# Chunk-selecting attention with a squared-ReLU feed-forward layer: x transposed by DMA in group 1, squares in pairs, keys placed after the bounds, a smaller causal mask

## The chip, the cores and the metric

The kernel runs on one core of one Trainium2 chip. The core has a matrix engine (TensorE, PE in the profile; its weight loads are shown apart as PEld), a vector engine (VectorE, DVE), a scalar engine (ScalarE, ACT), a general engine (GpSimd, POOL) and a queue engine (SyncE, SP). DMA transfers are issued from the queues of SP, ACT and POOL. Times are device microseconds (us) of the whole program; less is better.

## What is computed

Four sequences of 768 tokens with eight heads of 64 columns go through an attention that looks only at the best six chunks of keys for each query, and the result through a feed-forward layer with squared ReLU.

```python
k_min, k_max = min and max of k over each chunk of 32 keys
ub = sum over d of max(q * k_min, q * k_max)        # one bound per query and chunk
ub = where(chunk is not in the future, ub, -1e9)
top_chunks = the 6 chunks with the largest ub
scores = q @ k.T / 8, kept where the chunk is in top_chunks and the key is not in the future
attn = softmax(scores) @ v
x = attn with heads side by side                     # (3072, 512)
out = maximum(x @ w_in, 0) ** 2 @ w_out              # d_ff = 2048
```

## The kernel before

The work is cut into **groups** and **slots**. A group is one half (384 queries) of one sequence; `ORDER` lists the eight groups, half 0 of sequence 0, half 0 of sequence 1, half 1 of 0, half 1 of 1, then sequence 2 and 3 in order. A slot `s` is one pair of heads (`p` = 0 to 3) of one group, so slots 0 to 3 are group 0, slots 4 to 7 group 1, slots 8 to 11 group 2, and slot 31 is the last. In the code a group's number is `hb` or `g`, and `NP` is 4.

For each slot these steps run, spread over the slots before and after it:

- **step_P** (line 344) transposes keys and queries of the slot on PE (`tk`, `tq`, lines 251 and 258), from group 3 on it reads them from DMA transposes. **step_T2** (263) then makes the two relus of the query on ACT (`qr`, 279), the minimum and maximum of each key chunk on DVE (`extrema`, 218 to 226, into `kbd`) and **places** keys and queries in the operands of the scores (`place`, 281 to 285, `kq`): keys on DVE, queries on ACT.
- **step_U** (353) makes the bounds on PE: a matmul that adds the causal mask (359: identity times `cmask`, 144 columns in a second half, 48 in a first half), then two small matmuls per query block (363). DVE takes the eight largest bounds of each row (MAX8, 370) and writes which chunks fall short of the sixth (`chosen`, `nsel` or `qn`, 371).
- **step_V** (397) brings these choices into the query operand: transposes on PE into `qt` (404, 416), then copies by DVE (410; in slots 4 to 11 one copy for each of the two heads, 421). From slot 13 on **step_W** (390) does it by one DMA transpose issued from SP.
- **step_E** (424) computes scores of a head on PE (`ps`, 434) and their exponential on ACT (`e`, 440); POOL clears the causal triangle (444). **step_F** (450) multiplies by V (`po`, 460) and divides on DVE (`r`, `x`, 469 and 470). From group 2 to group 6 it also issues a DMA transpose of `x` from SP (474) into `xT`.
- Groups 0, 1 and 7 transpose `x` on PE instead (`x_T`, 492 to 501, tile `pt`) and copy it (`x_copy`, 504). For group 1 this stands in slot 8 (two sets of six transposes, g = 0 and 1), for group 7 in **step_X** (506) behind the last slot.
- **push** (513) puts a group's feed-forward pieces in a queue: 16 **ups** (`ffn_up`, 544: four matmuls `ph` against `w_in`, 547; a relu on ACT into `ht`, 551; a square on DVE into `h`, 553) and 12 **downs** (`ffn_down`, 556: four matmuls `py`, 563; each reads four of the 16 `h`). The main loop takes pieces from the queue by `f1()` at fixed places, four in each of slots 4 to 7 and six to eight in each later slot, so that PE has matmuls while the attention steps wait.

Every engine works its instructions off in program order; the order is written out by hand in two loops at the end, one for slots 0 to 3 and one for slots 4 to 31. Tables `later` (`at`, line 583), `first` and `by_sp` say at which slot a load or a DMA transpose is issued. Loads from HBM go through POOL's queue, in the order `at` gives: behind slot 0 both halves of `w_in`, behind slot 1 V of sequence 1, then keys and queries of group 2, then both halves of `w_out`.

Of the kernel before, what the change touches and what calls it, by code (L numbers as in the profile page):

```python
# [8 lines left out]
F32 = mybir.dt.float32  # L9
# [30 lines left out]
def kernel(  # L40
# [131 lines left out]

    cmask = consts.tile([128, HT, 2, NC], BF16, tag="cmask", name="cmask")
    nc.vector.memset(cmask, 0.0)
    for g in range(4):
        for j in range(HT):
            c = 13 + g + 4 * j
            if c < NC:
                nc.vector.memset(cmask[g * 32:(g + 1) * 32, j, :, c:NC], NEG)

# [172 lines left out]
    def step_U(s):  # L353
        b, half, p = slots[s]
        st[s]["e"] = [None, None]
        ncs = 12 * (half + 1)
        j0 = 1 - half
        ub = psA.tile([128, HT - j0, 2, ncs], F32, tag="att", name="ub")
        nc.tensor.matmul(ub, lhsT=ident, rhs=cmask[:, j0:, :, NC - ncs:NC],
                         start=True, stop=False)  # L360
        for j in range(j0, HT):
            for w in range(2):
                nc.tensor.matmul(  # L363
                    ub[:, j - j0], lhsT=st[s]["qr"][:, w, 128 * j:128 * (j + 1)],
                    rhs=kbds[b % 2][:, p, w, :, 0:ncs], start=False,
                    stop=(j == HT - 1 and w == 1))
        m8 = work.tile([128, HT, 2, 8], F32, tag="m8", name="m8")
        for j in range(j0, HT):
            for hh in range(2):
                nc.vector.max(out=m8[:, j, hh, :], in_=ub[:, j - j0, hh, :])  # L370
        nc.vector.tensor_tensor(
            (qn0[:, j0:, p, :, D:D + ncs] if s < NP else
             chosen[s % 2][:, j0:, :, 0:ncs] if s < ON_PE * NP else
             nsel[half][:, s % 2, :, j0:, 1, 0:ncs].rearrange("p h j c -> p j h c")),
            ub, m8[:, j0:, :, TOPK - 1:TOPK].to_broadcast([128, HT - j0, 2, ncs]),
            op=ALU.is_lt)
# [20 lines left out]
    def step_V(s):  # L397
        b, half, p = slots[s]
        if s < NP or s // NP >= ON_PE:

            qt = psA.tile([128, 2, HB], BF16, tag="att", name="qt")
            for hh in range(2):
                for j in range(HT):
                    nc.tensor.matmul(
                        qt[0:KR, hh, 128 * j:128 * (j + 1)],
                        lhsT=(qn0[:, j, p, hh, :] if s < NP else
                              nsel[half][:, s % 2, hh, j].rearrange("r n d -> r (n d)")
                              [:, 0:KR]),
                        rhs=ident, is_transpose=True, start=True, stop=True)
# [40 lines left out]
    def step_F(s, hh):  # L450
# [13 lines left out]
        if hh == 1:  # L464
            if p == 0:
# [14 lines left out]
    downs = []  # L480
    h2 = {}

    xTs = {}
# [22 lines left out]
    def step_X(hb, pe):  # L506
        if pe:
            for g in range(2):
                x_T(hb, g, A)
                x_copy(hb, g, 0, 2, nc.scalar.copy if g else nc.vector.tensor_copy)  # L510
        push(hb)

# [31 lines left out]
    def ffn_up(hb, xT, f):  # L544
        ph = psF.tile([128, 512], F32, tag="ph", name="ph")
        for ki in range(NKI):
            nc.tensor.matmul(  # L547
                ph[:, 0:HB], lhsT=w_in[:, ki, 128 * f:128 * (f + 1)],
                rhs=xT[:, ki, :], start=(ki == 0), stop=(ki == NKI - 1))
        ht = late.tile([128, HB], BF16, tag="ht", bufs=4, name="ht")  # L550
        nc.scalar.activation(ht, ph[:, 0:HB], ACT.Relu)  # L551
        h = late.tile([128, HB], BF16, tag="h", bufs=2 * NFI + 2, name="h")
        nc.vector.tensor_mul(h, ht, ht)  # L553
        h2[hb, f] = h

# [42 lines left out]
    at(0, codes, 1, 0, nc.gpsimd.dma_start)  # L598
    for g in range(2):
# [110 lines left out]
    for s, (b, half, p) in enumerate(slots):  # L710
# [32 lines left out]
        if s == 2 * NP:  # L743
# [7 lines left out]
            step_F(s - 1, 1)  # L751
            f1()
            f1()
            x_T(1, 1, F)
            x_copy(1, 1, 0, 2, nc.scalar.copy)
            push(1)
            extrema(st[s + 1]["k"], s + 1)
            place(s + 1, "k", nc.vector.tensor_copy)
        if p == 0 and hb > 2:
            step_F(s - 1, 0)  # L760
            step_F(s - 1, 1)
            step_X(hb - 1, False)
        else:
# [82 lines left out]
    fill(4, True)  # L846
    step_X(2 * B - 1, True)
    queue.extend(downs)
# [33 lines left out]
```

## Time and profile before

| | us |
|---|---|
| three runs: median (lowest to highest) | 270.51 (270.15 to 272.39) |
| the execution that was profiled | 270.16 |
| its span, first to last instruction | 268.4 |
| PE busy | 257.3 (96%) |
| ACT busy | 179.7 (67%) |
| DVE busy | 162.3 (60%) |
| POOL busy | 90.6 (34%) |

The granted clock of TensorE was 0.999 of full speed. A line of the timeline reads: start, length, engine, line of the code, operation, what it writes and reads, how many instructions are taken together; in brackets stands how long the engine idled before it and what ended that. A line of instructions taken together starts with the first and ends with the last, and one instruction may still be in its pipeline when the next begins; the step from start to start is what it holds its engine. That matters on PE, where a matmul's length in the profile is longer than the step to the next one. In the 40 slices a digit is the busy share in tenths; a slice is 6.7 us.

### The profile page before, as it was taken

How to read it: one execution, taken by the hardware profiler on the slowest of the kernel's cores; microseconds unless marked ns; L12 is line 12 of the kernel's file. 1: busy time of each engine (PE TensorE's matmuls, PEld its weight loads, DVE VectorE, ACT ScalarE, POOL GpSimd, SP SyncE). 2: the span in 40 equal slices, each digit the busy share in tenths (PEclk: the TensorE clock that was granted, in tenths of full speed). 3: DMA queues.
4: the chain of work that ended last, by engine and by line, in shares of the span. 5: the costliest groups of instructions: out<-in, count | busy, mean ns of one | idle time of the engine just before them, and what ended most of it. 6: DMA issues, size and time to landing. Idle time of an engine off the chain costs nothing.

```text
span 268.4 us, 6678 instructions
## 1 busy us (share of the span) xinstructions
PE 257.3 (96%) x2463; PEld 160.2 (60%) x2463; DVE 162.3 (60%) x627; ACT 179.7 (67%) x401; POOL 90.6 (34%) x135
## 2 busy tenths in 40 slices
PE   7888998999999999999999999999999999999995
PEld 6666565556666566655665566745565666655543
DVE  6778999666997458646875676555863233413411
ACT  5887889688976578845575777935685688525500
POOL 8695356425641425235521544320121111000000
PEclk9999999999999999999999999999999999999999
DMA  7999999959996799999995999997642210111112
GB/s 139 156 207 210 168 212 195 110 71 145 141 154 126 128 182 142 123 177 141 190 148 118 116 178 141 122 173 155 123 101 65 63 32 0 43 39 39 42 39 79
DMA packets 113057, 33.10 MB, mean 123 GB/s; under 512 B 99968, under 2 KB 108960, under 8 KB 113024
## 3 DMA queue, kind: packets, MB, share of 16 engines
q0 software_dynamic: 64592, 13.83, 68.9%
q1 hardware_dynamic: 47488, 18.44, 36.9%
q10 hardware_dynamic: 944, 0.39, 0.6%
q8 instruction: 19, 0.31, 0.5%
q14 instruction: 14, 0.11, 0.1%
HBM read 27.26 MB, written 6.29 MB: 125 GB/s over the span
## 4 chain that ended last, share of the span: by engine, by line
PE 78%; DVE 12%; ACT 3%; DMA 3%; issue 1%; SPq 1%; POOL 0%; DVEq 0%; POOLq 0%; ACTq 0%
PE py L563 28%; PE ph L547 25%; PE ps L434 11%; PE po L460 7%; DMA kqT<-kn 3%; PE idle L640 2%; PE ub L363 2%; DVE km L327 2%; DVE h L553 1%; PE py L535 1%; DVE m L370 1%; DVE km L222 1%; DVE kq L284 1%; DVE km L223 1%; DVE x L470 1%
## 5 line engine op out<-in xcount | busy, mean ns | idle before, releaser
L440 ACT ACTIVATE e<-ps 128x512 bf16<-128x512 f32 x192 | 96.5, 551 | 18.9 <-PE ps L434 18.3
L547 PE MATMUL ph<-xT,w_in 128*128 128x384 bf16 x512 | 98.7, 325 | 0.1
L563 PE MATMUL py<-w_out,h 128*128 128x512 bf16 x368 | 87.9, 379 | 0.2
L553 DVE TENSOR_TENSOR h<-ht 128x384 bf16<-128x384 bf16 x128 | 46.7, 375 | 55.3 <-ACT ht L551 55.0
L551 ACT ACTIVATE ht<-ph 128x384 bf16<-128x384 f32 x128 | 62.5, 501 | 25.2 <-PE ph L547 24.2
L444 POOL TENSOR_SCALAR_AFFINE_SELECT e<-e 128x384 bf16<-128x384 bf16 x64 | 34.0, 537 | 130.6 <-ACT e L440 127.0
L547 PEld LDWEIGHTS <-w_in 128*128 128x128 bf16 x512 | 47.6, 97 | 30.6 <-issue 1.3
L434 PE MATMUL ps<-kq 96*128 96x384 bf16 (+2 forms) x320 | 57.0, 277 | 1.7 <-DVE kq L410 1.3
L563 PEld LDWEIGHTS <-h 128*128 128x128 bf16 x368 | 34.8, 97 | 35.3 <-issue 0.6
L434 PEld LDWEIGHTS <-kq 96*128 96x128 bf16 x320 | 26.4, 97 | 16.2 <-issue 1.9
L569 ACT COPY ob<-py 128x512 f32<-128x512 f32 x19 | 11.1, 585 | 27.1 <-PE py L563 26.7
L370 DVE MAX8 m<-ub 128x8 f32<-128x24 f32 (+1 forms) x160 | 16.7, 171 | 18.8 <-PE ub L363 18.4
L460 PEld LDWEIGHTS <-e 128*128 128x128 bf16 x672 | 25.3, 98 | 4.0
L460 PE MATMUL po<-vn,e 128*128 128x65 bf16 x672 | 26.6, 194 | 0.0
L470 DVE TENSOR_TENSOR x<-po,r 128x384 bf16<-128x384 f32 x32 | 17.8, 557 | 1.1
L109 POOL DMA_DIRECT2D kn<-in_k_dram x15 | 13.3, 894 | 2.3 <-DMA kqT<-kn 2.2
L109 POOL DMA_DIRECT2D qn<-in_q_dram x15 | 13.4, 900 | 0.4 <-DVE km L327 0.2
L327 DVE TENSOR_TENSOR km<-km 128x384 bf16<-128x384 bf16 (+3 forms) x40 | 11.6, 290 | 1.1
L363 PE MATMUL ub<-kbd,qr 128*128 128x48 bf16 (+1 forms) x160 | 9.7, 180 | 1.4 <-DVE kbd L224 0.7
L125 POOL DMA_DIRECT2D vn<-in_v_dram x12 | 10.7, 902 | 0.3 <-issue 0.3
L640 PE MATMUL idle<-ident 128*128 128x128 bf16 x97 | 8.3, 246 | 2.2 <-POOL ident masks.py:199 1.4
L363 PEld LDWEIGHTS <-qr 128*128 128x128 bf16 x160 | 7.7, 96 | 4.4 <-DVE qr L307 1.2
(72 smaller groups left out, 185.6 us busy)
## 6 DMA issues: line engine op xcount, KB each, us to landing
out_dram<-ob SPq DMA_DIRECT2D x23, 256.0 KB, 2.4
w_in<-in_moe_w_in_dram POOLq DMA_DIRECT2D x2, 1024.0 KB, 11.8
w_out<-in_moe_w_out_dram POOLq DMA_DIRECT2D x2, 1024.0 KB, 18.2
kn<-in_k_dram POOLq DMA_DIRECT2D x15, 128.0 KB, 5.9
qn<-in_q_dram POOLq DMA_DIRECT2D x15, 128.0 KB, 5.9
kq<-kqT SPq DMA_DIRECT2D x10, 192.0 KB, 3.8
vn<-in_v_dram POOLq DMA_DIRECT2D x12, 128.0 KB, 9.4
vn<-in_v_dram POOLq DMA_DIRECT2D x4, 384.0 KB, 7.9
```

Source lines behind the costliest of these rows:

```text
L109: nc.gpsimd.dma_start(out=nat_of(n, g)[:, DM * j:DM * j + DM].rearrange("p (h d) -> p h d", d=D), in_=rows(n, *ORDER[g], 0, H)[:, 128 * j: ...
L363: nc.tensor.matmul(ub[:, j - j0], lhsT=st[s]["qr"][:, w, 128 * j:128 * (j + 1)], rhs=kbds[b % 2][:, p, w, :, 0:ncs], start=False, stop=(j ...
L370: nc.vector.max(out=m8[:, j, hh, :], in_=ub[:, j - j0, hh, :])
L434: nc.tensor.matmul(ps[:, at:at + 128 * m], lhsT=kqs[b % 2][0:KR, p, 2 * (j // HT), hh, 128 * (j % HT):128 * (j % HT + 1)], rhs=qc(s, hh)[: ...
L440: nc.scalar.activation(e[:, 512 * n + lo:512 * n + hi], ps[:, lo:hi], ACT.Exp, scale=float(scale))
L444: nc.gpsimd.affine_select(out=d, in_=d, compare_op=ALU.is_ge, fill=0.0, base=0, channel_multiplier=-1, pattern=[[0, 3], [1, 128]])
L460: nc.tensor.matmul(po[:, hh, i, :], lhsT=t["e"][hh][:, c:c + 128], rhs=vn[b % 2][:, 2 * p + hh, j, :], start=(j == 0), stop=(j == iq))
L470: nc.vector.tensor_mul(x[:, p].rearrange("p j (h d) -> p h j d", h=2), po[:, :, :, 0:D], r.to_broadcast([128, 2, HT, D]))
L547: nc.tensor.matmul(ph[:, 0:HB], lhsT=w_in[:, ki, 128 * f:128 * (f + 1)], rhs=xT[:, ki, :], start=(ki == 0), stop=(ki == NKI - 1))
L551: nc.scalar.activation(ht, ph[:, 0:HB], ACT.Relu)
L553: nc.vector.tensor_mul(h, ht, ht)
L563: nc.tensor.matmul(py[t], lhsT=h2[hb, f][:, 128 * t:128 * (t + 1)], rhs=w_out[:, f, :], start=(f == 0), stop=(f == NFI - 1))
```

## The change

In the order of the program:

- **Mask.** `cmask` shrinks from 24 to 4 columns per block and head. step_U runs the bounds first and adds the mask last, on the four chunks of the diagonal alone (24 columns in a second half, 16 in a first half); MAX8 reads only the chunks up to the diagonal.
- **V.** The three loads of V for sequence 1 are issued before the second half of `w_in`.
- **Choices.** In slots 4 to 6 each head's choices are transposed apart (four transposes instead of two), so that one copy on DVE brings both heads.
- **Squares.** The relu writes straight into `h`, and the square is made in place. `h` tiles hold two ups. In group 0 one instruction squares both; the first four pairs at once (slots 4 and 5), the other four pairs only in slot 8, behind the first two downs in program order. In later groups each up is squared by itself.
- **Keys.** For slots 6, 7 and 8 the keys are placed behind step_U's choice of that slot, where they had been placed behind the extrema, in front of the MAX8. The queries of slot 8 are placed by DVE instead of ACT.
- **x of group 1.** step_F issues the DMA transpose for slots 4 to 7 too; the twelve PE transposes and two copies in slot 8 go, and push(1) comes before two downs.
- **Slot 12.** Its choices go by step_W's DMA transpose, issued in slot 11 behind step_U(12), in place of six PE transposes and a copy on DVE.
- **Tail.** For group 7, three head pairs go by DMA transpose; only the last pair is transposed on PE (three transposes) and copied by DVE.

```diff
-    cmask = consts.tile([128, HT, 2, NC], BF16, tag="cmask", name="cmask")
+    cmask = consts.tile([128, HT, 2, 4], BF16, tag="cmask", name="cmask")
...
     def step_T2(s):
...
         if s >= NP:
-            place(s, "k", nc.vector.tensor_copy)
-            place(s, "q", nc.scalar.copy)
+            if s > 2 * NP:
+                place(s, "k", nc.vector.tensor_copy)
+            place(s, "q", nc.vector.tensor_copy if s == 2 * NP else nc.scalar.copy)
...
     def step_U(s):
-        nc.tensor.matmul(ub, lhsT=ident, rhs=cmask[:, j0:, :, NC - ncs:NC],
-                         start=True, stop=False)
+        bank = psA.tile([128, 192], F32, tag="att", name="ub")
+        ub = bank[:, 0:2 * nj * ncs].rearrange("p (j h c) -> p j h c", j=nj, h=2)
         for j in range(j0, HT):
...
+        c = 12 * half + 4 * j0
+        diag = bank[:, c:c + nj * (2 * ncs + 4)].rearrange("p (j x) -> p j x", j=nj)
+        nc.tensor.matmul(
+            diag[:, :, 0:2 * ncs].rearrange("p j (h c) -> p j h c", h=2)[:, :, :, 0:4],
+            lhsT=ident, rhs=cmask[:, j0:], start=False, stop=True)
...
-                nc.vector.max(out=m8[:, j, hh, :], in_=ub[:, j - j0, hh, :])
+                nc.vector.max(out=m8[:, j, hh, :],
+                              in_=ub[:, j - j0, hh, 0:12 * half + 4 * j + 4])
...
     def step_V(s):
-        if s < NP or s // NP >= ON_PE:
+        if s < NP:
...
+        if s < NP + 3:
+            qt = psA.tile([128, 2, HB], BF16, tag="att", name="qt")
+            for h in range(2):
+                for j in range(j0, HT):
+                    nc.tensor.matmul(
+                        qt[0:CR, h, 128 * j:128 * (j + 1)], lhsT=chosen[s % 2][:, j, h],
+                        rhs=ident, is_transpose=True, start=True, stop=True)
+            nc.vector.tensor_copy(
+                kqs[b % 2][D:KR, p, 2 * half + 1, :, c:], qt[0:CR, :, c:])
+            return
...
     def step_F(s, hh):
-            if 2 <= s // NP < 2 * B - 1:
+            if s // NP and s < NS - 1:
                 nc.sync.dma_start_transpose(
...
     def ffn_up(hb, xT, f):
-        ht = late.tile([128, HB], BF16, tag="ht", bufs=4, name="ht")
-        nc.scalar.activation(ht, ph[:, 0:HB], ACT.Relu)
-        h = late.tile([128, HB], BF16, tag="h", bufs=2 * NFI + 2, name="h")
-        nc.vector.tensor_mul(h, ht, ht)
-        h2[hb, f] = h
+        if f % 2 == 0:
+            two[hb] = late.tile([128, 2, HB], BF16, tag="h", bufs=NFI + 1, name="h")
+        h = two[hb]
+        x = h2[hb, f] = h[:, f % 2]
+        nc.scalar.activation(x, ph[:, 0:HB], ACT.Relu)
+        if hb:
+            nc.vector.tensor_mul(x, x, x)
+        elif f % 2 and f < NFI // 2:
+            nc.vector.tensor_mul(h, h, h)
+        elif f % 2:
+            squares.append(h)
...
-    for g in range(2):
-        at(0, load_w_in, 1024 * g, 1024 * g + 1024)
+    at(0, load_w_in, 0, 1024)
     for j in range(HT):
         at(1, load_vt, 1, j)
+    at(1, load_w_in, 1024, DFF)
...
         if s == 2 * NP:
-            x_T(1, 0, F)
-            x_copy(1, 0, 0, 2, nc.vector.tensor_copy)
             step_F(s - 1, 0)
             step_F(s - 1, 1)
-            f1()
-            f1()
-            x_T(1, 1, F)
-            x_copy(1, 1, 0, 2, nc.scalar.copy)
             push(1)
+            f1()
+            f1()
+            for h in squares:
+                nc.vector.tensor_mul(h, h, h)
             extrema(st[s + 1]["k"], s + 1)
             place(s + 1, "k", nc.vector.tensor_copy)
...
             step_U(s + (1 if hb < ON_PE else 2))
+        if NP < s < 2 * NP:
+            place(s + 1, "k", nc.vector.tensor_copy)
+        if s + 1 == ON_PE * NP:
+            step_W(s + 1)
...
-        if hb < ON_PE:
+        if s + 1 < ON_PE * NP:
             step_V(s + 1)
...
-    step_X(2 * B - 1, True)
+    x_T(2 * B - 1, 1, A, (1,))
+    x_copy(2 * B - 1, 1, 1, 2, nc.vector.tensor_copy)
+    push(2 * B - 1)
```

More of the change, by code (lines that the diff above doesn't have):

```diff
@@ L171 @@
     codes(0, 0, nc.sync.dma_start, 1, 2)
-    cmask = consts.tile([128, HT, 2, NC], BF16, tag="cmask", name="cmask")
+    cmask = consts.tile([128, HT, 2, 4], BF16, tag="cmask", name="cmask")
     nc.vector.memset(cmask, 0.0)
[L175 to L179, printed above, removed]
+    for g in range(3):
+        nc.vector.memset(
+            cmask[g * 32:(g + 1) * 32, :, :, g + 1:4].rearrange("p j h c -> p (j h) c"), NEG)
     hmask = consts.tile([128, 2, 2, 12], BF16, tag="hmask")
@@ L357, in step_U @@
         j0 = 1 - half
[L358 to L360 removed]
+        nj = HT - j0
+        bank = psA.tile([128, 192], F32, tag="att", name="ub")
+        ub = bank[:, 0:2 * nj * ncs].rearrange("p (j h c) -> p j h c", j=nj, h=2)
         for j in range(j0, HT):
@@ L364, in step_U @@
                     ub[:, j - j0], lhsT=st[s]["qr"][:, w, 128 * j:128 * (j + 1)],
-                    rhs=kbds[b % 2][:, p, w, :, 0:ncs], start=False,
-                    stop=(j == HT - 1 and w == 1))
+                    rhs=kbds[b % 2][:, p, w, :, 0:ncs],
+                    start=(j == j0 and w == 0), stop=False)
+        c = 12 * half + 4 * j0
[3 more added lines that the diff above has]
+            lhsT=ident, rhs=cmask[:, j0:], start=False, stop=True)
         m8 = work.tile([128, HT, 2, 8], F32, tag="m8", name="m8")
@@ L405, in step_V @@
                         qt[0:KR, hh, 128 * j:128 * (j + 1)],
-                        lhsT=(qn0[:, j, p, hh, :] if s < NP else
-                              nsel[half][:, s % 2, hh, j].rearrange("r n d -> r (n d)")
-                              [:, 0:KR]),
+                        lhsT=qn0[:, j, p, hh, :],
                         rhs=ident, is_transpose=True, start=True, stop=True)
@@ L481 @@
     h2 = {}
+    two = {}
+    squares = []
     xTs = {}
@@ L761 @@
             step_F(s - 1, 1)
-            step_X(hb - 1, False)
+            push(hb - 1)
         else:
```

8 lines of the change are left out of this document (1 added, 7 removed).

## The prediction

> **What bounds the kernel now.** I read the page first (the busy digits by slice), then the busy time by windows, then the timeline of TensorE (PE) and VectorE (DVE) in the windows where they differ, last the transfers.
>
> ```profile
> span 268.4 us, 6678 instructions
> PE   7888998999999999999999999999999999999995
> DVE  6778999666997458646875676555863233413411
> 31.00:48.00 17.00, 15.42 (x177) 9.79 (x176) 16.30 (x58) 14.51 (x36) 9.28 (x14) 1.00 1.60 195
> 84.00:268.40 184.40, 180.87 (x1551) 108.39 (x1547) 95.08 (x368) 112.64 (x243) 43.06 (x62) 1.00 0.85 108
> ```
>
> The digits show PE full from the eighth slice on, and DVE full in slices five to seven (27 to 47 us). The windows say the same in microseconds: from 31 to 48 us DVE is busy for 16.30 of 17.00 us and ScalarE (ACT) for 14.51; from 84 us to the end PE has 180.87 of 184.40 and DVE about half. So there are two regimes. Up to slot 8 (48 us) a shorter DVE chain can pay; behind it only work taken off PE pays, and a wait costs in full.
>
> **Slots 4 to 7.** The squares leave DVE here, keys are placed later, choices are copied at once. One round of DVE, in slot 5, with ACT's fifth and sixth relu under it:
>
> ```profile
> 32.58 1.12 DVE L284 COPY kq<-tk 64x384 bf16<-64x384 bf16 x2
> 33.62 0.66 DVE L553 TENSOR_TENSOR h<-ht 128x384 bf16<-128x384 bf16 x2
> 34.30 0.41 DVE L370 MAX8 m<-ub 128x8 f32<-128x12 f32 x4
> 34.87 0.35 DVE L553 TENSOR_TENSOR h<-ht 128x384 bf16<-128x384 bf16 x1
> 35.14 0.19 DVE L469 RECIPROCAL r<-po 128x6 f32<-128x6 f32 x1
> 35.83 0.35 DVE L553 TENSOR_TENSOR h<-ht 128x384 bf16<-128x384 bf16 x1
> 36.21 0.60 DVE L421 COPY kq<-qt 32x256 bf16<-32x256 bf16 x2
> 36.83 0.56 DVE L222 TENSOR_REDUCE km<-tk 128x12 bf16<-128x384 bf16 x1
> 33.38 0.50 ACT L551 ACTIVATE ht<-ph 128x384 bf16<-128x384 f32 x1
> 36.64 0.38 PE L434 MATMUL ps<-kq 96*128 96x384 bf16 x2
> 47.27 0.73 DVE L421 COPY kq<-qt 32x384 bf16<-32x384 bf16 x2
> 47.76 0.60 PE L434 MATMUL ps<-kq 96*128 96x384 bf16 x4 [0.37 <-DVE kq L421]
> L327 DVE TENSOR_TENSOR km<-kqT 128x768 bf16<-128x768 bf16 x10 | 5.7, 573 | 0.2 <-DMA kqT<-kn 0.2
> ```
>
> From start to start: two key copies 1.04 us, four squares 0.68 + 0.27 + 0.38 = 1.33, the two copies of choices 0.62. Slot 8's first scores (47.76) name the copy that DVE starts at 47.27, so what moves that copy moves everything behind.
>
> The edit looks like a relief, and I take most of it back. The pair's square in slot 5 needs both relus, and the second runs from 33.38 to 33.88: the bounds of slot 6 (MAX) stand behind it in DVE's queue, so they start near 34.4 as before (34.30). Before, DVE filled that wait with the keys (32.58); now these come behind the choice and in front of the division, the second pair and the copy of choices, for which the scores of slot 6 wait (36.64): they start about 1.0 us later. ACT's order does not move, so I see no earlier second relu. Then slots 6 and 7 lose all their squares and catch up. DVE's work between 33.9 and slot 8's copy: out go 1.0 of squares in slot 5 and 1.3 in each of slots 6 and 7 (-3.6); in come two pairs, 0.49 each (the 768-wide row's 573 ns less the 0.08 by which the next instruction starts before the end, as 32.58 + 1.12 overlaps 33.62), keys +1.04, slot 8's queries from ACT to DVE +1.04, the copy in slot 6 -0.16 (two of 0.31 against one of about 0.45), and, an estimate, 0.4 of waiting where DVE reaches slot 7's MAX before PE has its bounds: -3.6 + 0.98 + 1.04 + 1.04 - 0.16 + 0.4 = **-0.3**. Ends: -2.5 (ACT's slack, 17.00 - 14.51, if DVE held nothing) and +1.0 (the late scores never caught up). I take -0.3, being counted instruction by instruction. The six more transposes of choices lie in this DVE-bound stretch: nothing, at most 6 x 0.06.
>
> **Edits at nothing.** V sooner and w_in's second half three loads later on POOL's queue: the value sums and up matmuls of slots 5 and 6 are covered by the slots before them, no wait of PE names either, and I move these slots by no more than a few tenths; if slots 4 to 7 did shorten by microseconds, V would land late in the old order and w_in in the new, each at its own lateness in full. Squares in place (all later groups): ACT no longer waits for one of four relu buffers to be squared, but PE is full there, so ACT's wait is hidden behind it. The four transposes of x that SP now issues in slots 5 to 8 stand ahead of the first outputs, which nothing waits for; they share the DMA engines with the loads of w_out. Pushing group 1 before two downs leaves the queue's order as it was.
>
> **Slot 8.**
>
> ```profile
> 50.63 0.50 PE L498 MATMUL pt<-ident,x 128*128 128x128 bf16 x6
> 50.97 1.89 PE L563 MATMUL py<-w_out,h 128*128 128x512 bf16 x8
> 52.70 0.55 PE L434 MATMUL ps<-kq 96*128 96x128 bf16 x3
> 53.08 0.23 PE L359 MATMUL ub<-cmask,ident 128*128 128x144 bf16 x1
> 49.91 0.55 DVE L222 TENSOR_REDUCE km<-tk 128x12 bf16<-128x384 bf16 x1
> 50.95 0.18 DVE L224 TENSOR_TENSOR kbd<-hmask,km 128x48 bf16<-128x48 bf16 x1
> 58.57 0.81 PE L547 MATMUL ph<-xT,w_in 128*128 128x384 bf16 x4
> w_out<-in_moe_w_out_dram POOLq DMA_DIRECT2D x2, 1024.0 KB, 18.2
> 29.96 0.90 POOL L592 DMA_DIRECT2D w_out<-in_moe_w_out_dram  x1 [0.46 <-ACT ht L551]
> ```
>
> Two groups of six transposes of x go; the second held PE from 50.63 to 50.97, so 2 x 0.34 = **-0.7**. Four pairs of squares come, 4 x 0.49 = 1.96 us of DVE. Eight down matmuls take 1.73 (50.97 to 52.70), so the first of the sixteen began at 48.90; DVE was done with x and turned to the key extrema 1.0 later (49.91). From that start the pairs now end at +1.6, +2.1, +2.6 and +3.0, and PE wants them at +1.7, +2.2, +2.6 and +3.0: just covered. The extrema start at +3.0 instead of +1.0, the products are ready 1.2 later (49.91 to 50.95 + 0.18), at +4.2, and PE comes to the bounds of slot 9 0.38 behind the downs (53.08 - 52.70), at +3.85: **+0.3**. The copies off DVE and ACT relieve nobody here. The new transposes of x by DMA are first read by the up matmuls at 58.57, eight microseconds behind x: covered, bar a landing over 8 us. w_out's second half lands near 29.96 + 18.2 = 48.2, wanted at about 50.0: covered by 1.8.
>
> The Trainium skill (VectorE: DVE Perf Modes, Side-by-side) counts N/2 + 8 + about 150 cycles for such an op, which I estimate at 565 ns for 768 columns; the 573 ns row agrees in length. Were that also the distance from one to the next, the four would end 0.3 us later and the sum would give 269.1.
>
> **The mask on PE.**
>
> ```profile
> 88.77 0.23 PE L359 MATMUL ub<-cmask,ident 128*128 128x144 bf16 x1
> 88.83 0.31 PE L363 MATMUL ub<-kbd,qr 128*128 128x48 bf16 x6
> 88.99 0.38 PE L434 MATMUL ps<-kq 96*128 96x384 bf16 x2
> 77.66 0.23 PE L359 MATMUL ub<-cmask,ident 128*128 128x144 bf16 x1
> 78.01 0.47 PE L363 MATMUL ub<-kbd,qr 128*128 128x48 bf16 x6
> ```
>
> 144 columns take 0.06 us to the next instruction, 48 columns 0.16 / 6 = 0.026. The new mask has 24 columns: -0.04 in each of 16 slots of a second half. Where PE waits behind the mask (77.66 to 78.01; four such places) it was free and now follows the wait: +0.03. 12 x -0.04 + 4 x 0.03 = **-0.35**. In the first halves 16 columns replace 48, no gain; in slots 0 to 4, where MAX waits for the last bound, +0.03 each: **+0.1**. The narrower MAX and the shorter memsets run beside PE or before the first landing: 0.
>
> **Slot 12.** Its choices go by DMA.
>
> ```profile
> 79.80 0.31 DVE L371 TENSOR_TENSOR nsel<-ub,m 128x144 bf16<-128x144 f32 x1
> 81.01 0.50 PE L404 MATMUL qt<-ident,nsel 128*96 128x128 bf16 x6
> 84.49 0.60 PE L434 MATMUL ps<-kq 96*128 96x384 bf16 x4
> DMA to landing us min/median/max: 2.7/3.3/6.7
> kqT<-kn SPq DMA_TRANSPOSE x15, 4.5
> 78.09 0.35 SPq L573 DMA_DIRECT2D out_dram<-ob  x1
> ```
>
> Six transposes leave PE, 0.34 by slot 8's: **-0.3** (and a copy leaves DVE). SP has issued its output at 78.09 and waits for work, so the transpose starts when the choices are done, 79.80 + 0.31 = 80.1. PE wants it at 84.49 - 0.34 = 84.15, 4.0 us later. The kernel's other 19 transposes of this kind land after 2.7 to 6.7 us: 0 to +2.7. This one is issued while loads run, as those of kn are (median 4.5), so I take that row: **+0.5**.
>
> **The tail.**
>
> ```profile
> 236.05 0.83 PE L498 MATMUL pt<-ident,x 128*128 128x128 bf16 x12
> 236.89 3.61 PE L563 MATMUL py<-w_out,h 128*128 128x512 bf16 x16
> ```
>
> Twelve transposes hold PE for 0.84 us; three stay: **-0.6**. The other nine go by DMA, ahead of the ups by several microseconds of downs.
>
> **Sum.** -0.3 - 0.7 + 0.3 - 0.35 + 0.1 - 0.3 + 0.5 - 0.6 = -1.35, so -1.4. The profiled execution took 270.16 (span 268.4 and 1.8 around it), so 268.8; the median 270.51 is 0.35 above it, and against that the change is 0.6%.
>
> **Rivals.** (a) The reordered slots 4 to 7 give what ACT's slack allows, -2.5 instead of -0.3: 266.6. For it: DVE is the full engine there and sheds squares. Against: the relu at 33.38 ends a wait that no DVE edit shortens. (b) On the other side: the transpose of slot 12 lands late. At 6.7 us PE waits 2.7 instead of 0.5: 271.0; the kernel gets slower than before once the wait is 0.5 + 1.4 = 1.9, at a landing after 4.0 + 1.9 = 5.9 us. For it: a load-laden stretch, and one queue in order behind an output; against: a median of 3.3. The Trainium skill (VectorE: DVE Perf Modes, The three transpose paths) puts a 128x128 block at 1309 ns by DMA against 390 on TensorE; six blocks would be an estimated 7.9 us, a wait of 3.9 and 272.2. The trace differs on both: transposes on PE start 0.056 apart, and the longest six-block DMA took 6.7; so it changes no chance. (c) The change does not do what it says: the late scores of slot 6 are not caught up, +1.0 in place of -0.3, which swallows the gains elsewhere: 270.1. For it: the scores of slot 6 lose a full 1.0; against: 2.6 us of squares leave the two slots behind.
>
> **How the numbers follow.** Forecast 0.55, (a) 0.22, (b) 0.10, (c) 0.13. Predicted 268.8. The range 266.6 to 270.1 goes from (a) to (c) and leaves out (b) and a little beyond (a). About 1% (2.7 us) is what a measurement can tell from no change: faster means under 267.8, which is (a) and the lower edge of the forecast, 0.25; slower means over 273.2, the far end of (b), 0.04; the same 0.71.
>
> **What would show it.** After: a DVE wait for a relu ahead of slot 6's MAX, and scores of slot 6 some 1.0 us later than 36.64; slot 8's scores near 47.5; no transposes of x around 48 us, the bounds of slot 9 waiting for the key products; PE waiting under 1 us at slot 12's first scores; one step of -0.6 at the tail. I am wrong if slot 8's scores start before 46.5 (then (a)), or if one wait over 1.5 us stands on PE behind 48 us.

## The result, and the profile after

The changed kernel takes 271.52 us in the median (271.23 to 274.65), the kernel before, run beside it, 270.50. The ratio is 1.0038, with a 95% interval from 1.0024 to 1.0052: slower by 0.4%, where I forecast 0.6% faster. The profiled execution took 271.45 us with a span of 269.7, against 270.16 and 268.4: 1.3 us more.

The same digits of the page, for the kernel after:

```profile
span 269.7 us, 6557 instructions
PE   7878889899999999999999999999999999999995
DVE  5777879874997448545775567555863233413511
```

And its table of windows (length, then busy time of PE, PEld, DVE, ACT and POOL, each with its instructions):

```profile
31.00:48.00 17.00, 15.45 (x186) 9.80 (x185) 14.04 (x47) 14.06 (x35) 8.33 (x12) 1.00 1.54 197
84.00:269.70 185.70, 181.52 (x1562) 108.56 (x1562) 95.12 (x375) 112.72 (x244) 42.95 (x62) 1.00 0.79 109
```

Between 31 and 48 us DVE is busy 14.04 us instead of 16.30, as the change meant, and PE is no busier (15.45 against 15.42). DVE was relieved and PE got no more done in this window, so less work on DVE alone did not help; the distances below show where the time went instead.

To see where the time went I cut the run at the first matmul of the scores (`ps`) of each slot. From slot 1 on these distances repeat within 0.02 us from kernel to kernel where an edit doesn't touch them (only slot 12's moves by up to 0.2; the way to slot 1 varies by 0.3 among most kernels, so its +0.12 is not told from that), so they measure each part by itself. (They are differences of start times in the timeline of PE.)

| from scores of slot to slot | before | after | difference |
| --- | --- | --- | --- |
| start to 1 | 12.41 | 12.53 | +0.12 |
| 1 to 4 | 11.40 | 11.73 | +0.33 |
| 4 to 5 | 7.74 | 8.08 | +0.34 |
| 5 to 6 | 5.09 | 6.30 | +1.21 |
| 6 to 7, 7 to 8 | 5.33 + 5.80 | 4.97 + 5.36 | -0.80 |
| 8 to 9 | 11.46 | 11.77 | +0.31 |
| 9 to 31 | 165.69 | 165.53 | -0.16 |

The rest, from slot 31's scores to the end, is the same, though nine transposes left PE in the tail. The sum is +1.35. Slots 1 to 4, 4 to 5, 5 to 6 and 8 to 9 carry it, and the gain that I had forecast in the tail is missing; each of these shows in the timeline.

**Slots 1 to 4.** First PE's weight loads (PEld) and DVE ahead of slot 4's choices, before:

```profile
20.73 0.10 PEld L363 LDWEIGHTS <-qr 128*128 128x128 bf16 x1
...
20.95 0.18 DVE L224 TENSOR_TENSOR kbd<-hmask,km 128x48 bf16<-128x48 bf16 x1
...
21.19 0.25 PE L363 MATMUL ub<-kbd,qr 128*128 128x24 bf16 x4 [0.37 <-DVE kbd L224]
...
21.47 0.41 DVE L370 MAX8 m<-ub 128x8 f32<-128x12 f32 x4 [0.34 <-PE ub L363]
```

and after:

```profile
21.28 0.18 DVE L223 TENSOR_TENSOR kbd<-hmask,km 128x48 bf16<-128x48 bf16 x1
...
21.58 0.18 PEld L363 LDWEIGHTS <-qr 128*128 128x128 bf16 x4 [0.63 <-ACT qr L279]
...
21.61 0.25 PE L363 MATMUL ub<-kbd,qr 128*128 128x24 bf16 x4 [0.49 <-DVE kbd L223]
...
21.92 0.40 DVE L376 MAX8 m<-ub 128x8 f32<-128x8 f32 x4 [0.46 <-PE ub L370]
```

From the key products to MAX there are 0.52 us before (20.95 to 21.47) and 0.64 after. With the mask in front, the group's first weights (`qr`) were loaded at 20.73, ahead of the wait; without it the load stands behind the wait (21.58; `qr`, which the bracket names, had been done by 21.28) and the first bound starts 0.33 instead of 0.24 after the start of the products. That leaves 0.03 for the mask behind the bounds, the only part that I had counted.

**Slots 4 and 5**, DVE of the kernel after:

```profile
29.05 0.87 DVE L568 TENSOR_TENSOR h<-h 128x768 bf16<-128x768 bf16 x1
...
34.70 0.56 DVE L568 TENSOR_TENSOR h<-h 128x768 bf16<-128x768 bf16 x1 [1.84 <-ACT h L564]
35.18 0.39 DVE L376 MAX8 m<-ub 128x8 f32<-128x8 f32 x4
35.61 0.21 DVE L378 TENSOR_TENSOR chosen<-ub,m 128x48 bf16<-128x48 f32 x1
35.73 1.11 DVE L284 COPY kq<-tk 64x384 bf16<-64x384 bf16 x2
...
37.58 0.55 DVE L568 TENSOR_TENSOR h<-h 128x768 bf16<-128x768 bf16 x1
38.16 0.42 DVE L426 COPY kq<-qt 32x512 bf16<-32x512 bf16 x1
```

The wait for the second relu is there (1.84 us idle ahead of 34.70), and the keys (35.73) stand in front of the copy of choices. PE waits for it, and for more:

```profile
36.90 0.37 PE L257 MATMUL tk<-ident,kn 96*64 96x96 bf16 x8 [0.41 <-DVE kq L284]
...
38.63 0.39 PE L449 MATMUL ps<-kq 96*128 96x384 bf16 x2 [0.44 <-DVE kq L426]
...
48.49 0.37 PE L257 MATMUL tq<-ident,qn 96*64 96x96 bf16 x8 [0.82 <-DVE x L485]
```

The first and the last of these I had not foreseen. A key copy is also the last reader of a PSUM tile: while it is put off, PE can't transpose the next keys (36.90), and the division behind it keeps its own tile from the next queries (48.49).

**Slot 8.** DVE (with one row of POOL), then PE:

```profile
50.20 0.56 DVE L485 TENSOR_TENSOR x<-po,r 128x384 bf16<-128x384 f32 x1
50.65 0.52 POOL L459 TENSOR_SCALAR_AFFINE_SELECT e<-e 128x384 bf16<-128x384 bf16 x1 [2.06 <-ACT e L455]
50.68 2.31 DVE L770 TENSOR_TENSOR h<-h 128x768 bf16<-128x768 bf16 x4
52.91 0.55 DVE L221 TENSOR_REDUCE km<-tk 128x12 bf16<-128x384 bf16 x1
...
53.95 0.18 DVE L223 TENSOR_TENSOR kbd<-hmask,km 128x48 bf16<-128x48 bf16 x1
```

```profile
49.77 3.87 PE L579 MATMUL py<-w_out,h 128*128 128x512 bf16 x16
53.48 0.55 PE L449 MATMUL ps<-kq 96*128 96x128 bf16 x3
54.28 0.31 PE L363 MATMUL ub<-kbd,qr 128*128 128x48 bf16 x6 [0.25 <-ACT ob L585]
...
54.82 0.38 PE L449 MATMUL ps<-kq 96*128 96x384 bf16 x2 [0.22 <-DMA qn<-in_q_dram]
```

The bounds of slot 9 start at 54.28, right behind the key products of 53.95 + 0.18; the releasers in brackets (ACT's copy, a load of queries) are only the last events that the profile saw. PE's gap there is 0.41 us (54.28 - 53.48 - 3 x 0.13), and a second one of 0.36 follows ahead of 54.82. A third loss stands inside the downs: the sixteen take 3.71 us from the first to the scores behind them (49.77 to 53.48), where e6 below, which leaves no square for slot 8, takes 3.45. The first square runs beside a clearing on POOL and takes 0.90 us (50.68 to 51.58); one by one the four start at 50.68, 51.50, 51.97 and 52.44, and the down that reads the first of them starts at 51.63, 0.35 behind the one before it instead of 0.22.

**The tail**, PE and ACT:

```profile
237.39 0.33 PE L515 MATMUL pt<-ident,x 128*128 128x128 bf16 x3
238.22 3.61 PE L579 MATMUL py<-w_out,h 128*128 128x512 bf16 x16 [0.51 <-ACT ob L585]
```

```profile
237.59 0.58 ACT L585 COPY ob<-py 128x512 f32<-128x512 f32 x1 [3.78 <-PE py L579]
```

Nine transposes are gone, and the next downs wait until ACT has copied out the only `py` buffer (237.59 + 0.58 = 238.17). Before, the twelve transposes filled exactly this time.

### The profile page after: what moved, and what is told of

It is laid out like the page before. It is cut to its first block, busy times and chain, and to the rows that moved or that the text cites. A ratio compares the mean times of both kernels' runs of the same rounds, so it can differ in the third digit from the quotient of the medians.

```text
span 269.7 us, 6557 instructions
## 1 busy us (share of the span) xinstructions
PE 255.9 (95%) x2442; PEld 157.3 (58%) x2442; DVE 160.6 (60%) x608; ACT 177.4 (66%) x397; POOL 91.1 (34%) x135
## 4 chain that ended last, share of the span: by engine, by line
PE 77%; DVE 12%; ACT 7%; issue 2%; DMA 1%; POOL 0%; ACTq 0%; DVEq 0%; POOLq 0%
PE py L579 27%; PE ph L557 24%; PE ps L449 11%; PE po L475 7%; ACT e L455 3%; PE idle L656 2%; PE ub L363 2%; DVE km L327 2%; ACT h L564 2%; DMA qn<-in_q_dram 1%; PE py L545 1%; DVE m L376 1%; DVE kq L284 1%; ACT kq L284 1%; DVE x L485 1%
## 5 line engine op out<-in xcount | busy, mean ns | idle before, releaser
L564 ACT ACTIVATE h<-ph 128x384 bf16<-128x384 f32 x128 | 62.5, 500 | 26.7 <-PE ph L557 26.3
L566 DVE TENSOR_TENSOR h<-h 128x384 bf16<-128x384 bf16 x112 | 41.1, 375 | 56.9 <-ACT h L564 56.4
L376 DVE MAX8 m<-ub 128x8 f32<-128x16 f32 (+4 forms) x160 | 16.2, 168 | 18.2 <-PE ub L370 17.8
L363 PEld LDWEIGHTS <-qr 128*128 128x128 bf16 x160 | 8.3, 96 | 7.9 <-DVE qr L307 2.2
```

Source lines behind the costliest of these rows:

```text
L363: nc.tensor.matmul(ub[:, j - j0], lhsT=st[s]["qr"][:, w, 128 * j:128 * (j + 1)], rhs=kbds[b % 2][:, p, w, :, 0:ncs], start=(j == j0 and w ...
L376: nc.vector.max(out=m8[:, j, hh, :], in_=ub[:, j - j0, hh, 0:12 * half + 4 * j + 4])
L564: nc.scalar.activation(x, ph[:, 0:HB], ACT.Relu)
L566: nc.vector.tensor_mul(x, x, x)
```

## The experiments

My theory after this reading: each part of the change is priced by the wait it makes or uncovers, and the keys' new place costs most. The rival: the transfers (V's loads moved, three sets of DMA transposes) or the 768-wide squares cost it, wherever the keys stand. No experiment leaves out or changes any part of what is computed.

**e1: the mask ahead again** (whole 144 columns, MAX over all).

```diff
+        nc.tensor.matmul(ub, lhsT=ident, rhs=cmask[:, j0:, :, NC - ncs:NC],
+                         start=True, stop=False)
...
-        nc.tensor.matmul(
-            diag[:, :, 0:2 * ncs].rearrange("p j (h c) -> p j h c", h=2)[:, :, :, 0:4],
-            lhsT=ident, rhs=cmask[:, j0:], start=False, stop=True)
```

> The changed kernel with the mask as it was before: the whole 144 columns as the first matmul of each group of bounds, MAX over all of them. Theory 1 (the start is a chain PE - DVE - PE, and the mask behind the bounds lengthens each link): slot 4's first scores return from 24.26 us to about 23.8, and the later slots lose the 0.16 us that the short mask gave; the time is 271.5 - 0.45 + 0.15 = about 271.2. Theory 2 (the start is late because the loads of V, moved ahead, take transfers or the queue from the keys): slot 4's scores stay at 24.3 and the time is about 271.6.

271.75 us, ratio 1.0037 (0.9997 to 1.0076). The kernel before took 270.81 beside it, 0.31 more than in the result above, so the times can't tell 271.2 from 271.6. In the profiled execution the granted clock dipped in the second and third slice, and the way to slots 1 and 2 grew by it, so the start can be read only in part:

```profile
PEclk9889999999999999999999999999999999999999
```

From slot 2 to 4 it takes 8.08 us, as before, against 8.30. From slot 9 to 31 it takes 165.83 us against 165.53. The short mask is worth up to 0.30 us there (I said 0.35); 0.08 of it stands at slot 12, whose distance moves as much by itself. What the start costs in all was settled by e8, below.

**e2: keys placed where they were before**, ahead of the bounds, slot 8's queries on ACT again.

```diff
-            if s > 2 * NP:
-                place(s, "k", nc.vector.tensor_copy)
-            place(s, "q", nc.vector.tensor_copy if s == 2 * NP else nc.scalar.copy)
+            place(s, "k", nc.vector.tensor_copy)
+            place(s, "q", nc.scalar.copy)
...
-        if NP < s < 2 * NP:
-            place(s + 1, "k", nc.vector.tensor_copy)
```

> The changed kernel with the keys of slots 6 to 8 placed where they were before, ahead of the bounds, and slot 8's queries placed by ACT again. Theory 1 (DVE stands idle ahead of slot 6's MAX waiting for the second relu, and keys that used to fill this wait now stand in front of the copy of choices): slot 6's scores come 0.8 to 1.2 us sooner than 38.63, the waits of PE for kq and x in slots 5 to 7 go, slot 9's scores come 0.5 sooner than 60.73, and the time is about 271.0. Theory 2 (the pair, 768 columns at a stroke, is what delays the scores, wherever the keys stand): slot 6's scores stay within 0.3 of 38.6, and the time at 271.5.

270.22 us, ratio 0.9984 (0.9955 to 1.0012); its profiled execution is 1.43 shorter than that of the kernel after. Slot 5 to 6 takes 5.34 us (6.30), 7 to 8 takes 4.70 (5.36). DVE in slot 5:

```profile
32.77 1.11 DVE L283 COPY kq<-tk 64x384 bf16<-64x384 bf16 x2
34.69 0.56 DVE L567 TENSOR_TENSOR h<-h 128x768 bf16<-128x768 bf16 x1 [0.82 <-ACT h L563]
35.28 0.40 DVE L375 MAX8 m<-ub 128x8 f32<-128x8 f32 x4
...
37.12 0.42 DVE L425 COPY kq<-qt 32x512 bf16<-32x512 bf16 x1
```

The keys lie again in the time in which DVE waits anyway: MAX starts 0.10 us later than after, the copy of choices 1.04 sooner. The waits of PE at 36.90, 38.63 and 48.49 are all gone. From slot 4 to 8 it takes 23.22 us instead of 24.70, so the new places cost 1.48 us, more than the whole loss. Of this 0.96 stands between slots 5 and 6, where only slot 6's keys had moved. The rest can't be split: between slots 7 and 8, e2 moves slot 8's keys and also takes its queries off DVE (44.50, 1.11 us in the kernel after). The rival falls for this part.

**e3: squares one by one and at once**, keys behind the bounds.

```diff
-        if hb:
-            nc.vector.tensor_mul(x, x, x)
-        elif f % 2 and f < NFI // 2:
-            nc.vector.tensor_mul(h, h, h)
-        elif f % 2:
-            squares.append(h)
+        nc.vector.tensor_mul(x, x, x)
```

> The changed kernel with group 0's squares one by one and at once, behind each relu; the keys stay behind the bounds. Theory 1 (waiting for the second relu is half of slot 5's loss; deferring the other half only moves 2.3 us of DVE work into slot 8, where PE needs it): slot 6's scores come 0.3 to 0.6 sooner than 38.63, slots 7 and 8 lose this again because 2.6 us of squares return to slots 6 and 7, but slot 9's scores follow slot 8's by 11.4 instead of 11.8 us; slot 9's scores between 60.2 and 61.0, the time 271.0 to 271.8. Theory 2 (deferring is the part that gains, the keys' place alone loses): slot 8's scores later than 49.5 and the time above 272.

274.21 us, ratio 1.0131 (1.0077 to 1.0185). Theory 2 holds: with the keys late, deferring the squares is what keeps slots 6 to 8 short. (The edit also undoes the pairs; slot 5 to 6 takes 6.16 instead of 6.30 by that.) Slot 6 to 7 takes 5.35 instead of 4.97; behind it the clock of the profiled execution dips (the eighth slice below), and the lowest time, at full clock, is 273.03, 1.5 above the kernel after. Theory 1 had called deferring a mere move; it was worth more.

```profile
PEclk9999999799999999999999999999999999999999
```

**e4: a second accumulator in the tail.**

```diff
-            if tail:
+            if tail or (hb == 2 * B - 2 and t == 1):
                 py[t] = psS.tile([128, DM], F32, tag="ps", name="py")
```

> The changed kernel with one of the last groups' outputs summed in a second accumulator: the four down matmuls groups that follow the last transposes of x take a buffer of the scores' pool instead of waiting until ACT has copied the only down buffer out. Theory 1 (the nine transposes taken off PE in the tail were cover for this copy, so PE now waits 0.67 us for it): the wait goes and the time is 0.6 us shorter, 270.9. Theory 2 (the tail waits for the transfer of x, and the copy's name in the profile is incidental): a wait of similar length stands elsewhere, in front of the ups, and the time stays at 271.5.

270.75 us, ratio 0.9995 (0.9974 to 1.0017), where the kernel after has 1.0038. From slot 31's scores to the end it takes 42.83 us instead of 43.49. PE in the tail:

```profile
233.68 3.62 PE L579 MATMUL py<-w_out,h 128*128 128x512 bf16 x16
237.13 0.33 PE L515 MATMUL pt<-ident,x 128*128 128x128 bf16 x3
237.30 3.62 PE L579 MATMUL py<-w_out,h 128*128 128x512 bf16 x16
```

The wait is gone, 0.66 us: the downs start 0.17 behind the transposes instead of 0.83.

**e5: e2 with the loads in the order of before.**

```diff
-    at(0, load_w_in, 0, 1024)
+    for g in range(2):
+        at(0, load_w_in, 1024 * g, 1024 * g + 1024)
     for j in range(HT):
         at(1, load_vt, 1, j)
-    at(1, load_w_in, 1024, DFF)
```

> Keys as before (e2) and also the loads on POOL's queue in the order of before. Theory 1 (with V moved ahead, POOL is free earlier in slot 4 and its clearing of e's upper triangle, 28.91 to 29.51, now runs under DVE's first pair of squares, 29.04, which takes 0.87 us where the other three take 0.55): the first pair takes 0.55 again, slot 5's scores come 0.3 us sooner than in e2 (32.33), and the time is 0.3 shorter, 269.9. Theory 2 (the pair is long for a reason of its own, the first instruction on this shape, or the loads): the pair stays at 0.87 and the time at 270.2. Theory 3 (the sooner V was worth something): slots 5 and 6 wait for V and the time is above 270.5.

269.79 us, ratio 0.9972 (0.9949 to 0.9994). POOL and DVE around 29 us, in e2 and in e5:

```profile
28.91 0.60 POOL L458 TENSOR_SCALAR_AFFINE_SELECT e<-e 128x384 bf16<-128x384 bf16 x1 [1.76 <-ACT e L454]
...
29.04 0.87 DVE L567 TENSOR_TENSOR h<-h 128x768 bf16<-128x768 bf16 x1
```

```profile
29.09 0.54 DVE L567 TENSOR_TENSOR h<-h 128x768 bf16<-128x768 bf16 x1
...
30.92 1.12 POOL L458 TENSOR_SCALAR_AFFINE_SELECT e<-e 128x384 bf16<-128x384 bf16 x2
```

With V loaded sooner, POOL isn't waiting behind loads when slot 4's weights `e` are ready, clears their triangle at once, and DVE's square takes 0.87 us beside it. With the old order POOL comes to it at 30.92 and the square takes 0.54. Slot 4 to 5: 7.76 instead of 8.08. So the earlier load cost 0.32 us, and no transfer was late. The Trainium skill (SBUF — State Buffer, SBUF: two separate sides) says that DVE and GpSimd share one pair of SBUF ports as an exclusive lock, which a DVE instruction with two SBUF inputs contends for with a GpSimd one that reads SBUF, and where the later instruction waits for the whole of the earlier one; by that the square would have ended 0.55 behind 29.51, at an estimated 30.06, and the trace has 29.91: it agrees within 0.15.

**e6: e2 with all pairs at once**, none left for slot 8.

```diff
-        elif f % 2 and f < NFI // 2:
+        elif f % 2:
             nc.vector.tensor_mul(h, h, h)
-        elif f % 2:
-            squares.append(h)
```

> Keys as before (e2), and all eight pairs of squares at once, none left for slot 8. Theory 1 (deferring pays: slots 6 and 7 are bound by DVE, and in slot 8 a part of the 2.3 us lies beside the down matmuls): slot 8's scores come 1.0 to 1.6 us later than e2's 47.47, slot 9's follow them by 10.8 to 11.3 instead of 11.8 us, the time is 270.2 + 0.3 to 1.0. Theory 2 (deferring is a loss, the squares stand in front of slot 9's key products, 1.0 us): slot 8's scores at most 0.5 later, slot 9's 0.5 sooner than 59.26, the time 269.7 or less.

270.37 us, ratio 1.0002 (0.9977 to 1.0026). Slots 6 to 8 take 1.27 us more than in e2 (5.25 + 5.81 against 5.09 + 4.70), slot 8 to 9 takes 10.79 instead of 11.78. Deferring gains 1.27 and gives back 0.99: theory 1, with a net of 0.28 by the distances, at the lower edge of what it said (the medians differ by 0.15).

**e7: e2 with the transposes on PE in all three places** (group 1's x in slot 8, slot 12's choices, the whole tail). The edit for slot 12 is the one shown at e13.

```diff
+            for g in range(2):
+                x_T(1, g, F)
+                x_copy(1, g, 0, 2, nc.scalar.copy if g else nc.vector.tensor_copy)
             push(1)
...
-    x_T(2 * B - 1, 1, A, (1,))
-    x_copy(2 * B - 1, 1, 1, 2, nc.vector.tensor_copy)
+    for g in range(2):
+        x_T(2 * B - 1, g, A)
+        x_copy(2 * B - 1, g, 0, 2, nc.scalar.copy if g else nc.vector.tensor_copy)
```

> Keys as before (e2), and the transposes back on PE in all three places: group 1's x in slot 8, the choices of slot 12, all of the last group's x in the tail. Theory 1 (in slot 12 and in the tail the removed transposes were cover for waits: the square and relu ahead of slot 13's bounds, the copy of the down sums): from slot 12's to slot 13's scores and in the tail the time is the same as in e2 within 0.15 us; in slot 8, where PE waits 0.4 and 0.36 us for the key products behind the squares, at most 0.3 is lost; total 270.2 + 0 to 0.4. Theory 2 (each removed block gained its time on PE and something else took it): 0.3 to 0.8 more in slot 8, 0.3 in slot 12, 0.6 in the tail, 271.4 or more.

270.97 us, ratio 1.0015 (1.0002 to 1.0029). Split: slot 8 to 9 12.53 against 11.78, +0.75; slot 11 to 12 9.23 in both, 0; the tail 0. Neither theory had it whole: slot 8's transposes were time on PE, the other two sets were cover. The tail of e7:

```profile
236.72 0.83 PE L525 MATMUL pt<-ident,x 128*128 128x128 bf16 x12
237.56 3.61 PE L589 MATMUL py<-w_out,h 128*128 128x512 bf16 x16
```

Nine transposes more, and no time more: the downs follow at once, where in the kernel after they waited.

**e8: a mix.** e5, the accumulator of e4, and the mask ahead of the bounds in slots 0 to 4 only.

```diff
+        head = s <= NP
+        if head:
+            nc.tensor.matmul(ub, lhsT=ident, rhs=fmask, start=True, stop=False)
...
+        if not head:
...
```

> Keys and loads as before (e5), the second accumulator in the tail (e4), and the mask ahead of the bounds in slots 0 to 4 but the short one behind them later. If the single losses add (0.44 for the mask at the start by e1, 0.65 for the tail by e4, 0.3 for the loads): 270.2 - 1.4 = 268.8. If the start's gain is swallowed by slot 5's wait for the second relu, or by the loads: 269.2 to 269.5.

268.77 us, ratio 0.9934 (0.9915 to 0.9954): faster than both kernels. The single losses add (268.8 was expected). From slot 1 to 4 it takes 11.39 us, as before, against 11.73 in e5: the mask behind the bounds cost 0.34 in these three slots, and PE's weight load and the bounds stand again as before:

```profile
20.95 0.10 PEld L373 LDWEIGHTS <-qr 128*128 128x128 bf16 x1
...
21.41 0.25 PE L373 MATMUL ub<-kbd,qr 128*128 128x24 bf16 x4 [0.37 <-DVE kbd L231]
```

**e9, e10, e11, e12**: e8 with small edits. e9 squares slots 4 and 5 one by one; e10 leaves only slot 7's two pairs for slot 8; e11 takes slot 9's key extrema ahead of group 1's last division; e12 is e9 and e11.

```diff
e9  -        elif f % 2 and f < NFI // 2:
    -            nc.vector.tensor_mul(h, h, h)
    +        elif f < NFI // 2:
    +            nc.vector.tensor_mul(x, x, x)
e10 -        elif f % 2 and f < NFI // 2:
    +        elif f % 2 and f < 3 * NFI // 4:
e11 +            extrema(st[s + 1]["k"], s + 1)
                 step_F(s - 1, 0)
                 ...
    -            extrema(st[s + 1]["k"], s + 1)
                 place(s + 1, "k", nc.vector.tensor_copy)
```

> e8 with the squares of slots 4 and 5 one by one, the later ones still left for slot 8. Theory 1 (a pair can't begin before its second relu, so half of it that used to be done in the wait now stands ahead of slot 6's bounds): MAX of slot 6 and its scores come 0.2 us sooner, and the time is 268.6. Theory 2 (one instruction of 768 columns is cheaper than two of 384, and slot 5 is late for the choices' single copy): slot 6's scores 0.1 to 0.3 later, 268.8 to 269.1.

268.81 us, ratio 0.9953 (0.9921 to 0.9985). Slot 5 to 6 takes 5.19 us instead of 5.34: the pair's wait costs 0.15. Slot 4 to 5 takes 7.83 instead of 7.76. So 0.08 is left, which no time here can tell from nothing.

> e8 with only the two pairs of slot 7 left for slot 8, the two of slot 6 at once. By e6 the four pairs cost 1.26 us up to slot 8's scores when done at once and 1.0 in slot 8 when deferred. If both costs halve: 0.6 later at slot 8's scores, 0.5 regained by slot 9's, 268.9. If slot 6 has room on DVE (in e6 slot 7's scores came only 0.16 later): slot 8's scores 0.2 later, 0.5 regained, 268.5.

268.40 us, ratio 0.9941 (0.9909 to 0.9972). Slot 6 to 7 takes 0.16 more, 7 to 8 the same, 8 to 9 takes 0.54 less: the second case. Slot 6 had room for its two pairs.

> e8 with the extrema and products of slot 9's keys ahead of group 1's last division and ahead of the deferred squares, in a stretch of 1.1 us in which DVE idles. Theory 1 (in slot 8 PE waits 0.41 us for key products that stand behind the squares, and then for the scores' buffers behind ACT): the wait ahead of slot 9's bounds goes, slot 9's scores come 0.4 to 0.8 sooner, 268.0 to 268.4. Theory 2 (the wait belongs to ACT's copy of the down sums, which the profile names): no change, 268.8.

268.27 us, ratio 0.9923 (0.9905 to 0.9940). Slot 8 to 9 takes 11.06 instead of 11.78: theory 1. PE in slot 8, both gaps gone:

```profile
51.22 0.55 PE L461 MATMUL ps<-kq 96*128 96x128 bf16 x3
51.60 0.31 PE L373 MATMUL ub<-kbd,qr 128*128 128x48 bf16 x6
51.76 0.17 PE L382 MATMUL ub<-cmask,ident 128*128 128x24 bf16 x1
51.81 0.38 PE L461 MATMUL ps<-kq 96*128 96x384 bf16 x2
```

But slot 11 to 12 grows from 9.06 to 9.89. SP and PE there:

```profile
78.46 1.24 SPq L412 DMA_TRANSPOSE kq<-nsel  x1
...
83.67 0.60 PE L461 MATMUL ps<-kq 96*128 96x384 bf16 x4 [0.59 <-DMA kq<-nsel]
```

The gain of slot 8 is given back to slot 12's transfer, which lands 5.07 us behind its issue (78.46 to 83.53).

> e9 and e11 together: if both reasons hold and add, 0.2 + 0.4 to 0.8 below e8: 267.8 to 268.2; if the start of slot 9 is set by ACT, 268.6.

268.10 us, ratio 0.9916 (0.9901 to 0.9931). Slot 5 to 6 5.20, slot 8 to 9 11.06, slot 11 to 12 9.72: both reasons hold, and slot 12 takes most of it.

**e13: e12 with slot 12's choices on PE again.**

```diff
-        if s + 1 == ON_PE * NP:
-            step_W(s + 1)
...
-        if s + 1 < ON_PE * NP:
+        if hb < ON_PE:
             step_V(s + 1)
```

> e12 with slot 12's choices transposed by PE again. Open after e11 and e12: both lose in slot 12 most of what slot 9 gained. Theory 1 (the DMA transpose of slot 12's choices lands between 83.3 and 83.7 us however early it is issued, and has become the bound, the rival (b) of the prediction): slot 12's scores come 0.5 to 0.8 sooner than e12's 83.41, 267.4. Theory 2 (the removed transposes were time on PE after all, and slot 12 waits for something else): 0 to 0.3 later, 268.1 to 268.4.

267.89 us, ratio 0.9906 (0.9874 to 0.9938), the lowest median of all, though the times don't tell it from e12's. Slot 11 to 12 is back at 9.23, and slot 12's scores come 0.43 sooner than in e12 (82.98 against 83.41), a little less than theory 1 had said. e10's edit was not tried together with this one. The wait on the transfer is gone, and so is the one ahead of slot 13's bounds that the kernel after has (first row; e13's second):

```profile
84.05 0.47 PE L363 MATMUL ub<-kbd,qr 128*128 128x48 bf16 x6 [0.38 <-DVE qr L307]
```

```profile
81.05 0.46 PE L373 MATMUL ub<-kbd,qr 128*128 128x48 bf16 x6
```

## Why the prediction was wrong, point by point

- **Slots 4 to 7, forecast -0.3: +0.74** (23.96 to 24.70 from slot 4's to slot 8's scores). This is the step that failed most, in its sentence "Then slots 6 and 7 lose all their squares and catch up". Its first half came true: the wait for the second relu, the keys between choice and copy, scores of slot 6 at 38.63 instead of 36.64, of which 0.79 was there at slot 5 and 1.2 arose here. But only 0.80 was caught up. I counted DVE's instructions as if the sum decided; the late keys also hold PSUM tiles, and PE waits for the tiles (36.90, 48.49). e2 gives the price, 1.48 us with slot 8's queries in it. So what came, in kind, is my rival (c), to which I gave 0.13; its price of +1.0 for these slots is above the +0.74 measured, and the time is beyond its 270.1 because other places lost too. With the keys in their old place the same slots take 23.22, and 22.90 with the old loads (e5): 1.06 less than before, which is the catch-up I had expected, and more.
- **"V sooner" at nothing: +0.32** in slot 4, by e5 (it is part of the +0.74). I named transfers as its cover, and no transfer was late; what came sooner was POOL's own work, beside DVE's square. (Undisturbed, a pair takes 0.54 or 0.55 us.)
- **The mask, slots 0 to 4, +0.1: +0.34 in slots 1 to 4** by e8 against e5, since the weight load had been hidden in the wait and I had counted the 16 columns only. In the second halves -0.35: -0.22 to -0.30 by e1 (without and with slot 12). Mechanism right, size nearly.
- **Slot 8, -0.7 and +0.3: -0.75 and +0.99**, by e7 and e6. The first was right. The second named the right wait and missed two others. The gap ahead of the bounds is 0.41; another of 0.36 follows it ahead of the next scores, and both go when the key products come sooner (e11, -0.72). And the downs, which I had as "just covered", wait 0.26 for the squares (3.71 us against 3.45 in e6), since the first square runs beside POOL's clearing. (In e2 the downs don't wait; there PE's value sums take 0.24 more than in e6, behind a clearing.) My 0.49 from one square to the next was nearly right: where no clearing runs, they follow each other by 0.47 (51.50, 51.97, 52.44). The 0.565 us per pair that I estimated from the Trainium skill (VectorE: DVE Perf Modes, Side-by-side) is close to the length of one (0.54 to 0.55 here), but it is not the distance to the next. The four did end about 0.3 us later than I had counted, as they would by that figure, but the cause is the clearing.
- **Slot 12, -0.3 and +0.5: +0.14** (9.17 to 9.31 with the long mask, e1; 9.23 with the short one). The sum came near by luck, and the difference is no larger than this distance moves by itself; neither term was right. PE's 0.34 became a wait at slot 13's bounds for the square and `qr` (e7: putting the transposes back costs nothing), and the transfer was on time (it landed 3.32 us behind its issue, at 84.86, ahead of the scores at 85.99). It landed too late only when slots 8 and 9 came sooner (e11, where PE waits 0.59, and e12): rival (b) was real, but hidden. Six blocks took 5.07 us in e11, below the 7.9 that I estimated by the Trainium skill's figure per block (VectorE: DVE Perf Modes, The three transpose paths).
- **The tail, -0.6: 0.** I took PE's busy time for its critical time. The twelve transposes covered the copy of `py`; e4 shows it by giving the downs another accumulator, e7 by putting the transposes back.

By place, measured less forecast: slots 4 to 7 0.74 + 0.3 = 1.04, slot 8 0.31 + 0.4 = 0.71, tail 0.6, slots 1 to 4 0.33 - 0.1 = 0.23, slots 9 to 31 -0.16 + 0.15 = -0.01, and 0.12 ahead of slot 1, in all 2.69. Of the 1.04, 0.32 is V's. The profiled execution stands 271.45 - 268.8 = 2.65 above the forecast, so nothing large is missing. Neither of the two signs by which I would have known that I was wrong came up: slot 8's scores start at 48.96, not before 46.5, and the longest wait of PE behind 48 us is 0.82. The one looked for a gain, the other for one large wait, and the loss is a sum of small ones.

## What to carry to other kernels

An instruction taken off a full engine saves time only if nothing else had to pass during it: look at which copy, load or wait ran beside it, and whether the next instruction there waits for a buffer that has a single copy. Putting an instruction off keeps its inputs' buffers too, so ask of each moved step who writes next into what it reads. An order in which an engine has something harmless to do ahead of a wait can hide a weight load behind that wait; take it away, and the load stands on the path.

## What the runs showed of the hardware

- A clearing on POOL and a square on DVE that begins under it don't run side by side: 0.87 us for 768 columns beside it, 0.54 without (e2 and e5). In the fifteen kernels of this case, all 17 squares of 768 columns that began 0.2 us or more ahead of the end of a clearing ended 0.40 to 0.41 us behind that end. Of those of 384 columns 302 ended 0.20 to 0.22 behind it; in the other ten it was the clearing that took long, 0.86 to 1.06 us instead of about 0.52. In e5 the second pair takes 0.70 us beside POOL's issue of a load (30.33); why, the runs don't show.
- Here the weight load ahead of a waiting matmul was done during the wait where the mask's matmul stood in front (20.73 against 21.19); where the wait stood on the first instruction of its group, load and matmul followed it, and the matmul came 0.09 us later.
- A six-block DMA transpose issued 0.86 us sooner (79.32 in e8, 78.46 in e11) landed 0.12 us sooner by its semaphore (83.65 and 83.53); in e10 one issued at 78.90 landed at 82.85. Why was not tried.
